# Retention followed by an RWKV channel mix: block 5 in 64-token chunks, keys turned and state summed in one pass, and a new order of all pieces

## The chip, the cores and the metric

The kernel runs on one core of a Trainium2 chip. The metric is the device time of one execution in microseconds (us). The five engines of the core run side by side, each through its own list of instructions in order, and wait for each other through semaphores: TensorE (PE, matrix products into the eight PSUM banks), VectorE (DVE), ScalarE (ACT), GpSimd (POOL) and SyncE (SP). POOL and SP issue most of the transfers here.

## What is computed

Cut to what matters, with B = 4 batches, H = 8 heads, S = 768 tokens, D = 64:

```python
gamma = 1.0 - 2.0 ** (-5.0 - np.arange(H))
for t in range(S):                                   # a recurrence for each head
    state = gamma * state + einsum('bhd,bhe->bhde', k[:, :, t], v[:, :, t])
    y[:, :, t] = einsum('bhd,bhde->bhe', q[:, :, t], state) / np.sqrt(D)
x = y.transpose(0, 2, 1, 3).reshape(B, S, H * D)     # 512 features a token
xk = mu_k * x + (1 - mu_k) * x_prev                  # x_prev: the token before
xr = mu_r * x + (1 - mu_r) * x_prev
k = np.maximum(xk @ w_k, 0)                          # 512 -> 1024
out = sigmoid(xr @ w_r) * ((k * k) @ w_v)            # 1024 -> 512
```

## The kernel before

The 3072 tokens are cut into twelve blocks of 256, three to a batch: blocks 0 to 2 are batch 0, 3 to 5 batch 1, and so on. The recurrence is done by chunks: inside a chunk as a masked score matrix times the values, from chunk to chunk through a 64x64 state for each head. Blocks of the table HALF (6 to 11) use 64-token chunks; blocks of WIDE (2 to 5) have 128 consecutive tokens as one tile, blocks 0 and 1 have tokens that alternate.

Nothing is scheduled by rule. The string ORDER (line 25) lists every piece of work as `code.block.part`, with `~v`, `~a`, `~p`, `~s` for DVE, ACT, POOL and SP, and `@` for the PSUM banks. The loop at the end of the kernel emits the pieces in that order, and each engine runs its own in that order. The codes that the text below uses:

- `lq`, `lk`, `lv`: load q, k, v of a block; `wk`, `wr`, `wv`: load the weights; `st`: store an output tile. Tiles of q, k and v lie in rings of four buffers, `vs` in a ring of three.
- `Tq`, `Tk` (PE) turn q and k; `Eq`, `Ek` (ACT) bring them out of PSUM. `turned_k` and `trans` have two forms: by 128-row tiles (blocks of WHOLE) or by 64x64 quarters.
- `vs` scales v by the decay (line 253). `S` (PE) makes the scores, `M` masks them on DVE (line 354, for half blocks line 347). `C` (PE) makes a chunk's state, `U` adds the carried state on DVE (line 419), `G` decays it for the next block (ACT).
- `I` and `J` (PE, line 441) multiply the carried states by q, `Y` (PE) the masked scores by v, all into the same two banks. For blocks that aren't wide, `Y` contains what `J` does. `D` on DVE (line 514, for half blocks line 507) brings the result to the buffer xT.
- `dx` (line 529) and `X` (lines 552, 558) make xk and xr: four `X.n.0.j` and four `X.n.1.j` for a block or a pair of blocks. Pairs (3, 4), (6, 7) and (9, 10) share their pieces.
- `K` (PE): xk times w_k, in pieces of 0.87 us; `Qa`, `Qb` (ACT): relu and square. `R` (PE): xr times w_r; `s` (ACT): sigmoid. `V` (PE): times w_v; `O` on DVE (line 630): product with the gate.
- `z` (PE): products of zeros into an unused bank, in the first 19 us only. `gy`: a table of decays that `D` multiplies by.

So `I.4` is the piece in which PE multiplies block 4's carried states by its q. It reads the result of `U.4.0`, the first DVE sum of block 4's state. `K.0.0` is the first piece of the channel mix.

The four lists that the change touches stand at the top of the kernel:

```python
HALF = (6, 7, 8, 9, 10, 11)
WHOLE = (0, 1, 2, 3)
WIDE = (2, 3, 4, 5)
```

Of the kernel before, what the change touches and what calls it, by code (L numbers as in the profile page):

```python
# [9 lines left out]
F16 = mybir.dt.float16  # L10
# [6 lines left out]
HALF = (6, 7, 8, 9, 10, 11)  # L17
# [15 lines left out]
K.0.2@1 Qa.0.0~a Qb.0.0~a Qa.0.2~a lq.3~p X.1.0.1~v X.1.0.3~v X.1.1.0~v Qa.0.1~a K.0.3@0 Qa.0.3~a
lk.3~p vs.2~v Tq.2@1 X.1.1.2~v K.1.3@6 K.1.0@0 C.2@7 U.2.0~v lv.3~p Eq.2~a S.2.1@23 M.2.1~v S.2.0@45
M.2.0~v Qb.0.3~a lv.4~p K.1.1@1 X.1.1.1~v Qa.1.0~a t.0.1.0~a K.1.2@7 I.2@23 Qb.0.1~a Qa.1.1~a wv.0~p
Qb.0.2~a Tq.4@01 Eq.4~a Y.2 Qa.1.3~a Qb.1.1~a X.0.1.3~v X.1.1.3~v R.1.1@4 Tk.4@01 Ek.4~a J.2 R.1.0@6
Qa.1.2~a s.1.0~a X.0.1.2~v X.0.1.1~v X.0.1.0~v R.0.1@5 s.0.1~a s.1.1~a R.0.0@7 s.0.0~a S.4.1@01
Qb.1.0~a D.2~v dx.2~v X.2.0.2~v X.2.0.0~v S.4.0@23 Tq.3@4 Eq.3~a X.2.0.1~v wv.1~p X.2.0.3~v Tk.3@7
lq.5~p Ek.3~a K.2.2@5 Qa.2.2~a K.2.3@4 M.4.1~v M.4.0~v Qa.2.3~a Qb.2.3~a lk.6~p S.3.1@67 M.3.1~v
S.3.0@01 vs.3~p C.3@23 U.3.0~a Qb.2.2~a K.2.1@4 Qa.2.1~a K.2.0@2 Qa.2.0~a I.3@45 lq.6~p vs.4~v  # L40
C.4@67 U.3.1~v X.2.1.1~v V.0.1.0@3 M.3.0~v V.1.0.0@2 G.3~a U.4.0~v I.4@01 X.2.1.3~v U.4.1~v J.3
Qb.1.3~a Y.4 Qb.2.0~a lk.5~p X.2.1.2~v X.2.1.0~v Y.3 D.3~v dx.3~v V.0.0.0@7 V.0.1.1 O.0.1~v Tq.5@45
J.4 D.4~v dx.4~v R.2.0@6 Qb.2.1~a V.0.0.1 O.0.0~v X.3.0.1~v Eq.5~a Qb.1.2~a V.1.0.1 X.3.0.2~v
O.1.0~v Tq.6@01 Eq.6~a Tk.6@45 Ek.6~a st.0.0~s lk.7~p st.1.0~s V.1.1.0@3 V.1.1.1 O.1.1~v s.2.0~a
# [36 lines left out]
"""
# [3 lines left out]
def kernel(  # L85
# [12 lines left out]
    nc = tc.nc  # L98
# [113 lines left out]
    def first(n):  # L212
        return n % NB == 0
# [586 lines left out]
```

## Time and profile before

| | |
|---|---|
| median of 3 runs | 153.35 us (153.19 to 153.39) |
| span of the profiled execution, first to last instruction | 151.4 us |
| PE busy | 143.4 us, 95% of the span |
| DVE busy | 127.8 us, 84% |
| ACT busy | 103.6 us, 68% |
| POOL busy | 55.3 us, 37% |
| granted PE clock | 1.000 |

The profile is of one execution, and the time of a run lies some 1.9 us above its span. A row of the timeline has the start, the length, the engine, the line, the tiles written and read, the shapes and the count of instructions; in brackets stands how long the engine was idle before it and what ended that. An instruction's own length is longer than its step: the next one starts before it ends, so steps are read from the starts of neighbouring rows.

### The profile page before, as it was taken

To read this page: it belongs to the slowest core of one execution; us is meant where nothing else is said; L and a number is where in the kernel's file an instruction comes from. 1 tells how busy PE (TensorE), PEld (TensorE's weight loads), DVE (VectorE), ACT (ScalarE), POOL (GpSimd) and SP (SyncE) were. 2 spreads that over 40 slices of the span, in tenths; PEclk is the share of its full clock that TensorE was granted. 3 is DMA by queue.
4 is the path that set the end of the run, shared out by engine and by line. 5 is a ranking of instruction groups with operands and counts; after the bars stand their busy time and mean duration, and the time that the engine had idled before them with its cause. 6 is when DMAs were issued, how large, how long until landed. Compare 5 with 4: busy or idle time off the path is not lost.

```text
span 151.4 us, 5541 instructions
## 1 busy us (share of the span) xinstructions
PE 143.4 (95%) x2426; PEld 82.8 (55%) x2426; DVE 127.8 (84%) x212; ACT 103.6 (68%) x195; POOL 55.3 (37%) x65
## 2 busy tenths in 40 slices
PE   7878799999999999999999999999999999999991
PEld 3345487757754554547465564548456444655450
DVE  7886999999989999999999999999799999400432
ACT  3565979899844795779567786999604756839420
POOL 7953998577957309996710000000000000000000
PEclk9999999999999999999999999999999999999999
DMA  5999999999999999999999019301000005500433
GB/s 140 219 229 197 207 231 192 168 251 212 196 167 202 233 262 107 256 300 198 231 173 126 7 38 283 105 35 45 0 4 0 4 0 211 205 0 0 148 133 139
DMA packets 45624, 22.16 MB, mean 146 GB/s; under 512 B 37400, under 2 KB 41248, under 8 KB 45600
## 3 DMA queue, kind: packets, MB, share of 16 engines
q0 software_dynamic: 38704, 14.42, 74.5%
q1 hardware_dynamic: 6592, 7.21, 14.3%
q8 instruction: 19, 0.31, 0.8%
q10 hardware_dynamic: 304, 0.18, 0.4%
q14 instruction: 5, 0.04, 0.1%
HBM read 24.16 MB, written 6.29 MB: 201 GB/s over the span
## 4 chain that ended last, share of the span: by engine, by line
PE 73%; DMA 12%; POOL 11%; issue 1%; DVE 0%; POOLq 0%
PE ps L624 27%; PE ps L572 14%; DMA v<-in_v_dram 12%; PE ps L612 12%; PE ps L582 8%; PE ps L278 3%; POOL q L235 3%; POOL k L230 2%; PE ps L441 2%; POOL vs L253 2%; POOL v L230 2%; PE ps L366 1%; PE ps L462 1%; PE ps L642 1%; PE ps L318 1%
## 5 line engine op out<-in xcount | busy, mean ns | idle before, releaser
L624 PE MATMUL ps<-wv,k2s 128*128 128x512 f16 x184 | 44.1, 380 | 0.0
L591 ACT ACTIVATE kr<-ps 128x512 f32<-128x512 f32 x48 | 27.9, 594 | 12.5 <-PE ps L582 6.5
L624 PEld LDWEIGHTS <-k2s 128*128 128x128 f16 x184 | 17.1, 98 | 18.9 <-ACT k2s L603 0.4
L630 DVE SCALAR_TENSOR_TENSOR os<-ps,rs 128x512 f32<-128x512 f32 x23 | 15.6, 684 | 11.9 <-ACT rs L618 9.4
L612 PE MATMUL ps<-wr,xr 128*128 128x512 f16 x96 | 23.5, 379 | 0.0
L582 PE MATMUL ps<-xk,wk 128*128 128x256 f16 x192 | 23.2, 273 | 0.0
L572 PE MATMUL ps<-xk,wk 128*128 128x512 f16 x96 | 23.0, 379 | 0.0
L618 ACT ACTIVATE rs<-ps 128x512 f32<-128x512 f32 x24 | 13.6, 597 | 12.9 <-PE ps L612 12.1
L230 POOL DMA_DIRECT2D k<-in_k_dram x20 | 17.8, 903 | 10.3 <-PE ps L384 6.7
L582 PEld LDWEIGHTS <-wk 128*128 128x128 f16 x192 | 18.1, 98 | 3.7
L241 ACT COPY qT<-ps 128x1024 f16<-128x1024 f16 (+1 forms) x13 | 12.3, 946 | 9.5 <-PE ps L278 7.8
L558 DVE SCALAR_TENSOR_TENSOR xr<-dx,mu,xT 128x256 f16<-128x256 f32 (+1 forms) x32 | 17.9, 577 | 0.1
L230 POOL DMA_DIRECT2D v<-in_v_dram x18 | 16.0, 911 | 3.6 <-DMA wr<-in_moe_w_r_dram 1.9
L558 DVE SCALAR_TENSOR_TENSOR xk<-dx,mu,xT 128x256 f16<-128x256 f32 (+1 forms) x32 | 17.0, 579 | 0.2
L354 DVE TENSOR_TENSOR a<-ps,c_sb 128x1024 f16<-128x1024 f32 (+1 forms) x14 | 14.6, 1066 | 0.9 <-PE ps L339 0.6
L603 ACT ACTIVATE k2s<-kr 128x512 f16<-128x512 f32 x24 | 14.8, 631 | 0.3
L612 PEld LDWEIGHTS <-xr 128*128 128x128 f16 x96 | 9.0, 97 | 10.7 <-issue 0.5
L572 PEld LDWEIGHTS <-wk 128*128 128x128 f16 x96 | 9.1, 98 | 10.5
L599 ACT ACTIVATE k2s<-kr 128x512 f16<-128x512 f32 x24 | 14.5, 627 | 0.3
L241 ACT COPY kT<-ps 128x1024 f16<-128x1024 f16 (+1 forms) x13 | 12.2, 945 | 2.2 <-PE ps L272 1.7
L529 DVE TENSOR_TENSOR dx<-xT 128x1024 f32<-128x1024 f32 x11 | 13.4, 1221 | 0.2
L253 DVE TENSOR_TENSOR vs<-v,csm_sb 128x1024 f16<-128x1024 f32 x10 | 12.2, 1217 | 0.2 <-DMA v<-in_v_dram 0.2
(73 smaller groups left out, 165.6 us busy)
## 6 DMA issues: line engine op xcount, KB each, us to landing
out_dram<-os SPq DMA_DIRECT2D x23, 256.0 KB, 2.4
v<-in_v_dram POOLq DMA_DIRECT2D x18, 256.0 KB, 7.7
q<-in_q_dram POOLq DMA_DIRECT2D x11, 256.0 KB, 8.4
k<-in_k_dram POOLq DMA_DIRECT2D x21, 128.0 KB, 8.8
v<-in_v_dram POOLq DMA_DIRECT2D x2, 512.0 KB, 7.2
wk<-in_moe_w_k_dram POOLq DMA_DIRECT2D x2, 512.0 KB, 10.4
wv<-in_moe_w_v_dram POOLq DMA_DIRECT2D x2, 512.0 KB, 10.4
wr<-in_moe_w_r_dram POOLq DMA_DIRECT2D x1, 512.0 KB, 8.7
```

The costliest lines, as they stand in the source:

```text
L230: e.dma_start(out=dst[:, :, i * D : i * D + D], in_=src[:, i * P : i * P + P].rearrange("h p d -> p h d"),)
L241: e.copy(out=out, in_=in_)
L253: e.tensor_tensor(out=VS(n), in0=V32(n).rearrange("p h (i d) -> p i h d", i=2), in1=gks[:, int(half(n) or wide(n)), :, :, None].to_broadca ...
L354: nc.vector.tensor_tensor(out=a_full(n)[:, i, :, j0:j1], in0=pairs(banks("S", n, i, j0))[:, :, j0:j1], in1=(below if wide(n) else causal[: ...
L558: nc.vector.scalar_tensor_tensor(out=XM[w](k)[:, j, t0:t1], in0=DX(k)[:, j, t0:t1], scalar=mu[:, w * NCO + j : w * NCO + j + 1], in1=x[:, ...
L572: nc.tensor.matmul(banks("K", n, g), lhsT=wk16[:, co, g * P : g * P + P], rhs=XM[0](k)[:, co, :], start=(co == 0), stop=(co == NCO - 1),)
L582: nc.tensor.matmul(pz[:, i, :], lhsT=wk16[:, co, fo * P : fo * P + P], rhs=XM[0](k)[:, co, m * TM + t0 : m * TM + t1], start=(i == 0 and c ...
L591: nc.scalar.activation(out=kr, in_=banks("K", n, g, *u), func=AF.Relu)
L603: nc.scalar.activation(out=K2(n)[:, w * g : w * g + w, t0:t1], in_=kr.rearrange("p a t -> p (a t)").rearrange("p (i t) -> p i t", i=w), fu ...
L612: nc.tensor.matmul(banks("R", n, tb), lhsT=XM[1](k)[:, co, t : t + P], rhs=wr16[:, co, :], start=(co == 0), stop=(co == NCO - 1),)
L624: nc.tensor.matmul(banks("V", n, tb), lhsT=K2(n)[:, fo, tb * P : tb * P + P], rhs=wv16[:, fo, :], start=(fo == 0), stop=(fo == NFO - 1),)
L630: nc.vector.scalar_tensor_tensor(out=OS(2 * n + tb), in0=banks("V", n, tb), scalar=1.0 / (KSC * KSC), in1=RS(2 * n + tb), op0=ALU.mult, op ...
```

## The change

Block 5 moves from WIDE to HALF, so it has four 64-token chunks. Block 4 is added to WHOLE, so its q and k are turned by 128-row tiles. For blocks 5 to 11 (MERGED) the pieces `Tk` and `C` are replaced by `TC.n.0` and `TC.n.1`: each k quarter is loaded once as the stationary operand, and an identity and the scaled v stream past it side by side (128 columns), so one product leaves the turned k and the state next to each other in fp32. `Ec` (two a block, ACT) takes the turned k out, `U` reads the state beside it. An identity stands ahead of each scaled v for that, which is three more small DVE instructions at the start.

A piece `w.n` (ACT) copies 16 elements of a row out of the banks of `I.n`, after `I.n` and ahead of `Y.n`, so that `Y.n` waits for the copy. The ring of gates has six buffers in place of four, that of outputs eight in place of four, xT two in place of three. ORDER is new from start to end; w_k comes in three parts (`wk.2.4`, `wk.1.2`, `wk.0.1`) in place of two.

```diff
-HALF = (6, 7, 8, 9, 10, 11)
+HALF = (5, 6, 7, 8, 9, 10, 11)
-WHOLE = (0, 1, 2, 3)
-WIDE = (2, 3, 4, 5)
+WHOLE = (0, 1, 2, 3, 4)
+WIDE = (2, 3, 4)
+MERGED = (5, 6, 7, 8, 9, 10, 11)
...
+    def VS(n):
+        return VI(n)[:, 1:].rearrange("p (i h) d -> p i h d", i=2)
...
-    VS = ring("vs_", 3, [2, H, D], F16)
+    VI = ring("vs_", 3, [2 * H + 1, D], F16)
...
-    RS = ring("rs_", 4, [dm], F32)
-    OS = ring("os_", 4, [dm], F32)
+    RS = ring("rs_", 6, [dm], F32)
+    OS = ring("os_", 8, [dm], F32)
...
+    def both(n, i):
+        return banks("TC", n, i).rearrange("p u (j x t) -> p u j x t", j=NJ, x=2)
+
+    def turned_state(e, n, i):
+        ps = both(n, i)
+        for j in range(NJ):
+            for u in range(2):
+                for a, h, jo, hp in heads(j):
+                    k = 1 + i * H + h
+                    x = slice(0, 2) if more(n) or not (u and i) else slice(0, 1)
+                    nc.tensor.matmul(
+                        ps[low(a), u, j, x], lhsT=K16(n)[low(u), h, i * D : i * D + D],
+                        rhs=VI(n)[low(u), 0 : k + 1 : k][:, x],
+                        start=(j == 0), stop=(j == NJ - 1), skip_group_check=True,
+                    )
+
+    def turned_k_part(e, n, i):
+        copy(
+            e, KT(n)[:, :, i].rearrange("c j (u p) -> c u j p", u=2), both(n, i)[:, :, :, 0],
+        )
...
+        if merged(n):
+            src = both(n, c // 2)[:, c % 2, :, 1]
...
+    def fence(e, n):
+        us = slice(0 if half(n) or not first(n) else 1, 2)
+        e.copy(out=fenced[:, us], in_=pairs(banks("I", n))[:, us, :, 0:C:W])
...
-    def load_wk(e, h):
-        f = slice(h * dff // 2, (h + 1) * dff // 2)
+    def load_wk(e, a, b):
+        f = slice(a * dff // 4, b * dff // 4)
```

The new order shows best on the instruction lists. First POOL, from the load of block 1's v on: `vs_1` is the scaling of block 1's v, which waits for that load, and everything below it is issued after it. Before:

```order
L235 DMA v32_1_71<-in_v_dram 128x8x128
L230 DMA k16_2_68<-in_k_dram 128x8x64 x2
L735 DMA wk16_127<-in_moe_w_k_dram 128x4x512 x2
L253 ISA
L253 TENSOR_TENSOR vs_1_75<-v32_1_71,csm_sb_121 128x1024
L235 DMA q16_2_64<-in_q_dram 128x8x128
L230 DMA v32_2_72<-in_v_dram 128x8x64 x2
L235 DMA q16_0_62<-in_q_dram 128x8x128
L738 DMA wr16_129<-in_moe_w_r_dram 128x4x512
L230 DMA k16_0_66<-in_k_dram 128x8x64 x2
```

And now:

```order
L244 DMA v32_1_71<-in_v_dram 128x8x128
L239 DMA v32_2_72<-in_v_dram 128x8x64 x2
L772 DMA wk16_133<-in_moe_w_k_dram 128x4x512
L262 ISA
L262 TENSOR_TENSOR vs_1_75<-v32_1_71,csm_sb_127 128x1024
L239 DMA k16_2_68<-in_k_dram 128x8x64 x2
L244 DMA q16_2_64<-in_q_dram 128x8x128
L772 DMA wk16_133<-in_moe_w_k_dram 128x4x256
L244 DMA q16_0_62<-in_q_dram 128x8x128
L772 DMA wk16_133<-in_moe_w_k_dram 128x4x256
L239 DMA k16_0_66<-in_k_dram 128x8x64 x2
L775 DMA wr16_135<-in_moe_w_r_dram 128x4x512
```

Block 2's k and half of w_k moved from ahead of the scaling to behind it; the load of block 3's v (`v32_3`) follows these rows directly. Further down POOL's list before there is a second scaling, that of block 3's v; now there is none.

Second DVE, from the last `dx` of batch 0 to `U.4.0`, which is the row that writes `tg2_1`. Before, from behind the four `X.2.0.j`:

```order
L354 TENSOR_TENSOR a2_1_84<-ps_61,c16_sb_120 128x1024 x2
L354 TENSOR_TENSOR a2_0_83<-ps_61,c16_sb_120 128x1024
L253 TENSOR_TENSOR vs_1_75<-v32_0_70,csm_sb_121 128x1024
L419 TENSOR_TENSOR t32_0_86<-ps_61,tg2_0_93 128x256
L558 SCALAR_TENSOR_TENSOR xr_2_106<-dx_0_99,mu_125,xT0_130 128x256
L354 TENSOR_TENSOR a2_0_83<-ps_61,c16_sb_120 128x1024
L419 TENSOR_TENSOR tg2_1_94<-ps_61,tg0_1_88 128x256
```

Now, from behind the first `X.2.0.j`:

```order
L262 TENSOR_TENSOR vs_0_74<-v32_3_73,csm_sb_127 128x1024
L363 TENSOR_TENSOR a2_1_84<-ps_61,c16_sb_126 128x1024
L594 SCALAR_TENSOR_TENSOR xk_2_103<-dx_0_99,mu_131,xT0_136 128x256 x3
L594 SCALAR_TENSOR_TENSOR xr_2_106<-dx_0_99,mu_131,xT0_136 128x256
L363 TENSOR_TENSOR a2_1_84<-ps_61,c16_sb_126 128x1024
L594 SCALAR_TENSOR_TENSOR xr_2_106<-dx_0_99,mu_131,xT0_136 128x256
L451 TENSOR_TENSOR t32_0_86<-ps_61,tg2_0_93 128x256
L262 TENSOR_TENSOR vs_1_75<-v32_0_70,csm_sb_127 128x1024
L363 TENSOR_TENSOR a2_0_83<-ps_61,c16_sb_126 128x1024
L594 SCALAR_TENSOR_TENSOR xr_2_106<-dx_0_99,mu_131,xT0_136 128x256 x2
L363 TENSOR_TENSOR a2_0_83<-ps_61,c16_sb_126 128x1024
L451 TENSOR_TENSOR tg2_1_94<-ps_61,tg0_1_88 128x256
```

The scaling of block 3's v (`vs_0<-v32_3`) has come over from POOL, and all four `xr_2` rows (the `X.2.1.j`) now stand ahead of `U.4.0`, where there was one.

On PE, the pieces that stand ahead of `I.4` are the same in both lists, with these exceptions: two `V` pieces (V.0.1.0 and V.1.0.0) were ahead of it and now follow it, `R.2.0` followed it and is now ahead, and the `z` pieces at the start are others. Ahead of `Y.0`, PE turns block 1's q and k in both lists; before, a `z` piece stood between the last score of block 0 and those turns, now none does. `Y.1` now follows directly on `I.1`, where the other half of block 1's scores, a turn and a `z` piece stood between them. `K.0.2` in place of `K.0.0` is the first piece of the channel mix.

More of the change, by code (lines that the diff above doesn't have):

```diff
@@ L164 @@
     wr16 = const.tile([P, NCO, dm], F16, name="wr16")
-    xT = [const.tile([P, NJ, COLS], F32, name=f"xT{b}") for b in range(B - 1)]
+    xT = [const.tile([P, NJ, COLS], F32, name=f"xT{b}") for b in range(2)]
     ident = c16[:, 0:P]
@@ L213, in first, with merged @@
         return n % NB == 0
+    def merged(n):
+        return n in MERGED
     def more(n):
@@ L406, in summed @@
     def summed(e, n, c):
[L407 to L410 removed]
+        last = c == (3 if half(n) else 1)
+        if merged(n):
+            src = both(n, c // 2)[:, c % 2, :, 1]
+        elif half(n):
+            src = banks("C", n)[:, c % 2, c // 2 * NJ * D : (c // 2 + 1) * NJ * D]
         else:
+            src = banks("C", n)
             src = (src[:, c] if more(n) else src)[:, 0 : NJ * D]
[L413 to L414 removed]
+        if not merged(n):
+            src = src.rearrange("p (j d) -> p j d", j=NJ)
         to = T32(n) if last else carried(n, c + 1)
@@ L677, in masks @@
             ((causal[:, 0], 1, ALU.is_ge), (causal[:, 1], 1, ALU.is_gt)),
-            ((step, 2, ALU.is_ge), (below, 0, ALU.is_ge)),
+            ((step, 2, ALU.is_ge), (below, 0, ALU.is_ge))
+            + tuple((VI(i)[:, 0], 2, ALU.is_equal) for i in range(3) if MERGED),
         )[part]:
```

128 lines of the change are left out of this document (62 added, 66 removed).

## Prediction

> **What bounds the kernel now.** I read the 40 slices of the page first, then the busy time by stretches, then the timelines of PE, DVE and POOL up to 43 us.
>
> ```profile
> PE   7878799999999999999999999999999999999991
> DVE  7886999999989999999999999999799999400432
> PEclk9999999999999999999999999999999999999999
> DMA  5999999999999999999999019301000005500433
> 13.95:42.59 28.64, 26.93 (x490) 18.86 (x489) 28.10 (x42) 25.66 (x50) 23.43 (x25) 1.00 1.50 206
> 42.59:148.24 105.65, 105.65 (x1757) 57.81 (x1756) 88.81 (x136) 70.72 (x131) 22.94 (x26) 1.00 0.71 123
> ```
>
> PE is full from about 19 us to the end, and at full clock. But DVE is full too, from slice 5 to slice 33, and the DMA engines are full up to 83 us. The last two rows are stretches (length, then the busy time of PE, PEld, DVE, ACT and POOL, the clock, DMA). From 13.95 to 42.59 us DVE is busy 28.10 of 28.64 us; from 42.59 on PE is busy all of 105.65 us and DVE has room. So a shorter PE list helps only behind the first stretch, and in the first stretch any added DVE work or DVE wait counts in full. The two limits are my stages, and the place where they hand over is `I.4`, which starts at 42.59 us:
>
> ```profile
> 41.90 0.42 DVE L419 TENSOR_TENSOR tg<-ps,tg 128x256 f16<-128x256 f32 x1 [0.20 <-ACT tg L424]
> 40.76 1.90 PE L624 MATMUL ps<-wv,k2s 128*128 128x512 f16 x8
> 42.59 0.42 PE L441 MATMUL ps<-qT,tg 64*64 64x128 f16 x12
> ```
>
> The first row is `U.4.0`; it ends at 42.32. PE has two V pieces until 42.59, then `I.4` and `J.3`. So the DVE chain and PE reach this point within 0.3 us of each other. The span ends 3.2 us after PE's last product at 148.24; the order of the last pieces (two V, a half-width V piece, its product with the gate, its store) is the same in kind, so I leave that, and the 1.9 us from span to median, as they are.
>
> **The start: D.0 comes about 0.55 us earlier.** These rows carry it (DVE, then PE, then POOL):
>
> ```profile
> 13.95 1.23 DVE L514 TENSOR_TENSOR xT<-ps,gy_sb 128x1024 f32<-128x1024 f32 x1 [1.19 <-PE ps L441]
> 10.87 1.89 DVE L354 TENSOR_TENSOR a<-ps,c_sb 128x512 f16<-128x512 f32 x3 [0.60 <-PE ps L339]
> 11.61 0.59 PE L710 MATMUL ps<-zero 128*128 128x512 f16 x2 [0.80 <-DVE a L354]
> 8.34 0.41 PE L272 MATMUL ps<-c_sb,k 128*64 128x128 f16 x8 [0.20 <-DMA k<-in_k_dram]
> 12.13 0.64 PE L272 MATMUL ps<-c_sb,q 128*64 128x128 f16 x16
> 12.60 0.61 PE L272 MATMUL ps<-c_sb,k 128*64 128x128 f16 x16
> 13.14 0.64 PE L489 MATMUL ps<-a,vs 64*64 64x128 f16 x32
> 4.65 0.90 POOL L235 DMA_DIRECT2D k<-in_k_dram  x1
> 5.52 0.92 POOL L235 DMA_DIRECT2D v<-in_v_dram  x1
> 13.66 1.90 POOL L253 TENSOR_TENSOR vs<-v,csm_sb 128x1024 f16<-128x1024 f32 x1 [3.98 <-DMA v<-in_v_dram]
> ```
>
> D.0 waits for `Y.0` (13.14 to 13.9), which stands behind `Tk.1` (12.60). In the new order the zeros ahead of `Tq.1` are gone, so `Tq.1` can run at about 11. `Tk.1` then waits for block 1's k. That load is issued just ahead of block 1's v, whose landing released POOL at 13.66; the second half of block 0's k landed at 8.3 (row at 8.34), and between then and 13.6 four loads (0.25, 0.5, 0.5 and 0.5 MB in HBM), so block 1's k lands one half-megabyte ahead, at about 12.1. Then `Tk.1` 0.54 us (12.60 to 13.14), `Y.0` and the way to DVE 0.81 (13.14 to 13.95): D.0 at 13.4. The three added identities and the late `gy` table lie on DVE while it waits anyway (0.20 us for v, 0.60, 1.19 in the rows of DVE); uncovered they would cost some 0.6 us.
>
> **From D.0 to U.4.0: DVE gets longer by 2.3 us.** One stretch of DVE without a wait gives all the steps, from start to start:
>
> ```profile
> 31.07 1.22 DVE L514 TENSOR_TENSOR xT<-ps,gy_sb 128x1024 f32<-128x1024 f32 x1
> 32.32 1.22 DVE L529 TENSOR_TENSOR dx<-xT 128x1024 f32<-128x1024 f32 x1
> 33.58 1.67 DVE L558 SCALAR_TENSOR_TENSOR xk<-dx,mu,xT 128x256 f16<-128x256 f32 x4
> 35.17 3.54 DVE L354 TENSOR_TENSOR a<-ps,c_sb 128x1024 f16<-128x1024 f32 x3
> 38.63 1.22 DVE L253 TENSOR_TENSOR vs<-v,csm_sb 128x1024 f16<-128x1024 f32 x1
> 39.76 0.42 DVE L419 TENSOR_TENSOR t<-ps,tg 128x256 f32<-128x256 f32 x1
> 40.09 0.48 DVE L558 SCALAR_TENSOR_TENSOR xr<-dx,mu,xT 128x256 f16<-128x256 f32 x1
> ```
>
> D 1.25, dx 1.26, X 0.40, M 1.15, vs 1.13, U 0.33. Before, from D.0 up to `U.4.0`: 3 D, 2 dx, 8 M, 2 vs, 4 U, 21 X = 3.75 + 2.52 + 9.20 + 2.26 + 1.32 + 8.40 = 27.45 us. The trace has 41.90 - 13.95 = 27.95, so waits made 0.5 of it. Now: the same, plus block 3's `vs` (1.13, which POOL did before, beside the rest) and three more `X.2.1.j` (1.20): 29.8 us. With the same half microsecond of waits, `U.4.0` starts at 13.4 + 29.8 + 0.5 = 43.7 and ends at 44.1, and `I.4` starts there. Without any wait it is 43.6.
>
> Does PE get there sooner by itself? Before, from `K.0.0` at 19.47 to `I.4` are 23.1 us. `K.0.2` should start near 19.05: D.0 at 13.4, two M, four X and one U are 4.25 us, so the last `X.0.0.j` ends near 18.9, and `Y.1` stands behind `I.1`, behind `w.1` and so behind `U.1.0`, which costs PE about half a microsecond there. From `K.0.2` to `I.4` the V pieces are missing (-1.83, 40.76 to 42.59), `Tk.2` is added (0.57, as 12.60 to 13.14), so is `R.2.0` (0.96), and block 4's two turns by 128-row tiles cost 0.5 each where quarters took 0.27 (+0.45): 23.25, so PE could be there at 42.3. That is 1.8 us before DVE, and PE must wait it out. This is also where PE's waits for late loads vanish: up to 1.8 us of them is covered.
>
> `I.4` thus moves from 42.6 to 44.1: +1.5 us.
>
> **From I.4 to the end: PE's list, about +0.4 us.** Ahead of `I.4` PE has lost two V pieces that now come behind it: +1.83. `R.2.0` is off this side, and block 5 is cheaper:
>
> ```profile
> 46.28 1.04 PE L612 MATMUL ps<-wr,xr 128*128 128x512 f16 x4
> 47.15 1.89 PE L624 MATMUL ps<-wv,k2s 128*128 128x512 f16 x8
> 55.94 0.62 PE L331 MATMUL ps<-qT,kT 64*128 64x128 f16 x16
> 56.49 0.32 PE L384 MATMUL ps<-vs,k 128*64 128x64 f16 x8
> 70.14 0.45 PE L318 MATMUL ps<-qT,kT 64*64 64x64 f16 x32
> 70.41 0.44 PE L462 MATMUL ps<-a,vs 64*64 64x64 f16 x32
> ```
>
> `R.2.0` is 0.87 (46.28 to 47.15). Block 5's scores go from 0.55 (55.94 to 56.49) to 0.27 (70.14 to 70.41); with its `Y`, `I` and `J` by the same pace I put the saving at 0.4 to 0.7. The merge: `Tk` and `C` of a half block are 32 products of 64 columns each, 0.27 each by the pace of these rows; `TC` is 32 products of 128 columns. The nearest row with 64x64 quarters and 128 columns is `Y.0`, 32 in 0.48 us (13.14 to 13.62). So 0.54 becomes 0.48 a block, six blocks (beside block 5): -0.4 at most, 0 if the two-piece moving operand costs anything. Sum: 1.83 - 0.87 - 0.55 - 0.2 = +0.2 by the middle values, between -0.15 and +0.6; each `TC` also stands alone among the large products more often than a `Tk` next to a `C` did, and each such switch of tile form costs PE about 0.1 us (four large products take 0.87 by the two rows at 46.28 and 47.15, so eight would take 1.74, while the eight ahead of `I.4` took 42.59 - 40.76 = 1.83). I take +0.4.
>
> The Trainium skill has another price for the merge: "TensorE: Matmul & The Clock Gate", under "Wait — 56ns, not 53.3ns?", says that starts of products never come closer than about 25 ns however few columns they have. By it 64 products would take 1.6 us and the merge would save 0.8 us a block. The trace disagrees: 32 products in 0.27 us are 8.4 ns each.
>
> The copies `w` cost PE nothing but at `Y.1`, since at least 0.5 us of other products stand between `I.n` and `Y.n`; on ACT they are twelve short copies, and `Ec` adds 14 copies of half size for 7 full ones, some 4 us in all on an engine that is busy 103.6 of 151 us. If they weren't covered, each would cost PE about 0.5 us, 5 in all at worst. The larger rings release DVE's products with the gate; DVE has room there, so nothing.
>
> **Sum.** 153.35 + 1.5 + 0.4 = **155.2 us**. Its own range is 154.2 (no waits on DVE, and the lower end behind `I.4`) to 156.2.
>
> **Rivals.** *DVE doesn't decide, PE does* (chance 0.17): `I.4` starts when PE is ready, at 42.3, by -0.3; behind it -0.15 to +0.6. That gives 152.9 to 153.7, and below 153.0 if `K.0.2` starts before 19. For it speaks that the two limits lie 0.3 us apart today; against it, the added 2.3 us are counted instructions with measured steps, and DVE had only 0.5 us of waits to lose. It decides if DVE covers D.0 to `U.4.0` in under 28 us. *Products paced by the instruction, not the column* (0.05): if a `TC` product keeps the 8.4 ns of a 64-column one, seven blocks save 0.27 each, 1.9 us: 153.3. Against it stands the row of `Y.0`, 15 ns each at 128 columns. *Late loads* (0.18, slower than my forecast): POOL's list behind block 1's scaling now holds block 2's k, the quarters of w_k, wr and then block 3's v.
>
> ```profile
> 15.51 0.95 POOL L235 DMA_DIRECT2D q<-in_q_dram  x1
> 16.45 1.79 POOL L230 DMA_DIRECT2D v<-in_v_dram  x2
> 19.07 0.82 POOL L738 DMA_DIRECT2D wr<-in_moe_w_r_dram  x1
> v<-in_v_dram POOLq DMA_DIRECT2D x18, 256.0 KB, 7.7
> ```
>
> The nine issues ahead of block 3's v take 0.75 to 0.95 each by these rows, so it is issued at 23.4 and 24.3 and lands 7.7 us later, near 32. DVE wants it after 3 D, 2 dx, 4 M, 1 vs, 3 U and 17 X, 19.8 us by the steps above, at 33.2. With the DMA engines full it may land 1 to 3 us later, and DVE then waits with everything behind it, for the whole 1 to 2 us: 156.2 to 157.5. It decides from a landing at 33.7 on. The rest (0.60) is the forecast.
>
> **Range and chances.** The likeliest is 155.2. The forecast's range with the late loads reaches 157.2 upward, and downward I take in most of the PE rival: 153.1 to 157.2. About 0.2 % (0.3 us) is what a measurement of this kernel can tell. Slower by more than that: all of the forecast, late loads, and a small part of the PE rival, 0.80. Within: 0.09, from the PE rival and the paced products. Faster: 0.11, from the same two.
>
> **What would show it.** In the changed kernel D.0 (the first DVE product with the `gy` table over 128x1024) near 13.4; from it to the DVE sum ahead of `I.4` 29.8 to 30.5 us with DVE nearly full; PE with 1.5 to 2.5 us of idle time between `K.0.2` (near 19) and `I.4` (near 44); PE full from there on, for about 106 us. A `TC` piece should take 0.23 to 0.25 us. I am wrong if `I.4` starts before 43, if PE idles more than 1 us behind it, or if D.0 is not near 13.4.

## The result, and the profile after

| | kernel before | changed kernel |
|---|---|---|
| median | 153.27 us of 4 runs (153.00 to 153.39) | 157.21 us of 4 runs (156.10 to 158.36) |
| ratio | 1 | 1.0249, 95% interval 1.0205 to 1.0293 |
| profiled execution | span 151.4 us | 157.17 us, span 155.4 us |
| PE busy | 143.4 us | 146.0 us |
| I.4 starts | 42.59 us | 46.12 us |
| from I.4 to PE's last product | 105.65 us | 105.96 us |

The changed kernel is 2.5% slower, by 3.9 us. Medians and ranges here and below are of all executions of a kernel, while a ratio leaves out those that lie over 1.5% above the fastest of their kernel (one of e2_vs3_on_pool, one of e9_first_of_before, two of e11_first_mended), so it need not be the ratio of two medians.

First the page of the changed kernel: busy time, then the slices (40 equal parts of the span) of PE, DVE, the granted clock and the transfers.

```profile
PE 146.0 (94%) x2260; PEld 82.6 (53%) x2260; DVE 128.7 (83%) x217; ACT 104.1 (67%) x214; POOL 55.9 (36%) x67
PE   7998765999999999999999999999999999999991
DVE  7897996989999999999999998999899995601242
PEclk9999999999999999999999999999999999999999
GB/s 142 214 224 231 129 134 174 206 211 252 206 197 228 165 203 60 295 193 223 158 218 172 126 292 6 6 104 35 4 4 0 0 79 128 0 202 0 202 101 169
```

The same row of transfer rates for the kernel before:

```profile
GB/s 140 219 229 197 207 231 192 168 251 212 196 167 202 233 262 107 256 300 198 231 173 126 7 38 283 105 35 45 0 4 0 4 0 211 205 0 0 148 133 139
```

Counted from 0, slices 4 and 5 (15.5 to 23.3 us) carry 129 and 134 GB/s where they carried 207 and 231. There the transfers have a hole, and PE has one right behind it, 6 and 5 tenths in slices 5 and 6. The busy times of the two stretches, from D.0 to I.4 and on to PE's last product (length, then PE, PEld, DVE, ACT, POOL, the clock, DMA share and rate), place the loss:

```profile
13.62:46.12 32.50, 28.34 (x457) 19.11 (x455) 30.12 (x46) 24.87 (x54) 25.12 (x28) 1.00 1.43 190
46.12:152.08 105.96, 105.96 (x1625) 57.47 (x1624) 87.49 (x135) 72.29 (x148) 22.90 (x26) 1.00 0.69 119
```

The first stretch took 28.64 us before and takes 32.50 now, and PE idles 4.2 us of it. Behind I.4 PE is full, for 0.3 us more. PE's timeline of the changed kernel says what it waited for:

```profile
19.55 1.92 PE L618 MATMUL ps<-xk,wk 128*128 128x256 f16 x16
21.40 0.64 PE L281 MATMUL ps<-c_sb,k 128*64 128x128 f16 x16
24.40 0.64 PE L281 MATMUL ps<-c_sb,q 128*64 128x128 f16 x16 [2.37 <-DMA q<-in_q_dram]
25.80 1.05 PE L618 MATMUL ps<-xk,wk 128*128 128x256 f16 x8 [0.76 <-DMA wk<-in_moe_w_k_dram]
45.16 1.02 PE L648 MATMUL ps<-wr,xr 128*128 128x512 f16 x4
46.12 0.42 PE L473 MATMUL ps<-qT,tg 64*64 64x128 f16 x12
```

It waited 2.37 us for block 2's q (Tq.2), then 0.76 us for w_k (K.0.1). DVE, which is the engine that the prediction watched, waits as well, behind PE:

```profile
27.21 0.42 DVE L451 TENSOR_TENSOR tg<-ps,tg 128x256 f16<-128x256 f32 x1 [1.47 <-PE ps L393]
31.95 1.22 DVE L546 TENSOR_TENSOR xT<-ps,gy_sb 128x1024 f32<-128x1024 f32 x1 [0.72 <-ACT kr L627]
```

The first row is U.2.0, which needs block 2's state, and that stood on PE behind the late pieces. The second is D.2. The view puts its wait down to ACT, but D.2 also needs J.2, which PE ran from 31.54 to 31.85 us. Why the loads are late stands in POOL's timeline:

```profile
8.16 0.83 POOL L772 DMA_DIRECT2D wk<-in_moe_w_k_dram  x1
14.12 1.90 POOL L262 TENSOR_TENSOR vs<-v,csm_sb 128x1024 f16<-128x1024 f32 x1 [5.13 <-DMA v<-in_v_dram]
15.97 1.82 POOL L239 DMA_DIRECT2D k<-in_k_dram  x2
17.76 0.90 POOL L244 DMA_DIRECT2D q<-in_q_dram  x1
18.63 0.79 POOL L772 DMA_DIRECT2D wk<-in_moe_w_k_dram  x1
```

From 9.0 to 14.1 us POOL waits for block 1's v, in order to scale it, and scales until 16.0. Everything below it is issued only then. What had been issued ahead has landed by 18.6 us, and the rate of the transfers falls meanwhile:

```profile
17.00:18.00 1.00, 1.00 (x6) 0.35 (x3) 1.00 (x3) 0.38 (x1) 1.00 (x2) 1.00 0.58 72
```

The last figure is 72 GB/s. In the kernel before, the same microsecond has 207.

### The profile page after: what moved, and what is told of

The parts are those of the page before. It is cut to its first block, busy times and chain, and to the rows that moved or that the text cites. A ratio compares the mean times of both kernels' runs of the same rounds, so it can differ in the third digit from the quotient of the medians.

```text
span 155.4 us, 5244 instructions
## 1 busy us (share of the span) xinstructions
PE 146.0 (94%) x2260; PEld 82.6 (53%) x2260; DVE 128.7 (83%) x217; ACT 104.1 (67%) x214; POOL 55.9 (36%) x67
## 4 chain that ended last, share of the span: by engine, by line
PE 74%; DMA 10%; POOL 5%; DVE 5%; ACT 3%; issue 1%; POOLq 0%
PE ps L660 26%; PE ps L608 14%; PE ps L648 11%; PE ps L618 10%; DMA v<-in_v_dram 5%; DMA wk<-in_moe_w_k_dram 5%; PE ps L422 3%; PE ps L473 2%; POOL q L244 2%; PE ps L494 1%; PE ps L327 1%; ACT qT L250 1%; PE ps L287 1%; POOL k L239 1%; PE ps L678 1%
## 5 line engine op out<-in xcount | busy, mean ns | idle before, releaser
L618 PE MATMUL ps<-xk,wk 128*128 128x256 f16 x192 | 24.3, 273 | 0.9 <-DMA wk<-in_moe_w_k_dram 0.8
L648 PE MATMUL ps<-wr,xr 128*128 128x512 f16 x96 | 24.0, 379 | 0.0
L239 POOL DMA_DIRECT2D v<-in_v_dram x20 | 18.0, 918 | 9.8 <-DVE vs L262 7.1
L262 DVE TENSOR_TENSOR vs<-v,csm_sb 128x1024 f16<-128x1024 f32 x11 | 13.4, 1218 | 0.5 <-DMA v<-in_v_dram 0.5
L244 POOL DMA_DIRECT2D q<-in_q_dram x12 | 10.7, 894 | 5.8 <-PE ps L287 4.9
L363 DVE TENSOR_TENSOR a<-ps,c_sb 128x1024 f16<-128x1024 f32 (+1 forms) x12 | 12.2, 1040 | 0.2 <-PE ps L348 0.2
```

The costliest lines, as they stand in the source:

```text
L239: e.dma_start(out=dst[:, :, i * D : i * D + D], in_=src[:, i * P : i * P + P].rearrange("h p d -> p h d"),)
L618: nc.tensor.matmul(pz[:, i, :], lhsT=wk16[:, co, fo * P : fo * P + P], rhs=XM[0](k)[:, co, m * TM + t0 : m * TM + t1], start=(i == 0 and c ...
L648: nc.tensor.matmul(banks("R", n, tb), lhsT=XM[1](k)[:, co, t : t + P], rhs=wr16[:, co, :], start=(co == 0), stop=(co == NCO - 1),)
```

## Experiments

Each ran beside fresh runs of the kernel before, whose medians lay between 153.26 and 153.37 us.

| | median, us | range | ratio to before, 95% |
|---|---|---|---|
| e1_loads_ahead | 154.67 | 154.37 to 155.21 | 1.0085 (1.0067 to 1.0103) |
| e2_vs3_on_pool | 156.97 | 155.78 to 159.33 | 1.0218 (1.0176 to 1.0260) |
| e3_both | 154.48 | 154.36 to 154.77 | 1.0066 (1.0049 to 1.0082) |
| e4_k2_late_in_before | 159.40 | 159.05 to 160.97 | 1.0401 (1.0367 to 1.0434) |
| e5_prefix | 155.41 | 154.88 to 156.98 | 1.0157 (1.0117 to 1.0197) |
| e7_zeros | 159.67 | 159.48 to 160.51 | 1.0422 (1.0402 to 1.0442) |
| e10_zeros_sized | 158.16 | 157.92 to 158.22 | 1.0321 (1.0303 to 1.0338) |
| e8_zeros_in_after | 157.29 | 156.97 to 157.59 | 1.0257 (1.0240 to 1.0274) |
| e12_zeros_in_after_sized | 156.23 | 156.14 to 158.29 | 1.0213 (1.0167 to 1.0258) |
| e9_first_of_before | 159.02 | 157.94 to 161.84 | 1.0346 (1.0313 to 1.0380) |
| e11_first_mended | 156.44 | 155.62 to 159.07 | 1.0176 (1.0145 to 1.0207) |

### The three loads, and the scaling of block 3's v

```diff
-lv.2~p wk.2.4~p t.0.0.3~a z.2@0 S.1.1@45 vs.1~p M.1.1~v ... M.1.0~v lk.2~p
-z.5@1 C.1@01 ... w.1~a lq.2~p Y.1 ... X.0.0.0~v wk.1.2~p
+lv.2~p wk.2.4~p lk.2~p lq.2~p wk.1.2~p t.0.0.3~a z.2@0 S.1.1@45 vs.1~p M.1.1~v ... M.1.0~v
+z.5@1 C.1@01 ... w.1~a Y.1 ... X.0.0.0~v
```

> The changed kernel, with three loads (block 2's k, block 2's q, the second part of w_k) moved on POOL from behind the scaling of block 1's v to ahead of it; nothing else differs. Theory (late loads): the scaling waits for block 1's v until 14.0 us, so these loads are issued only from 16.0 on and land at 21.1, 24.4 and 25.8 us; PE waits 2.6 us for block 2's q and 1.0 us for w_k. Issued some 6 us earlier they land before PE asks for them, PE reaches I.4 as early as DVE's list lets it, near 44.2 us in place of 46.1, and the time falls from 157.2 to about 155.3. Rival (DVE's longer list alone makes the loss, and PE's waits are covered): I.4 stays within 0.5 us of 46.1 and the time within 0.5 us of 157.2. Second rival (the transfers only change places: what is pulled ahead pushes block 1's v back): the scaling ends later than 17 us, block 1's state is late, and the time gains less than 0.8 us.

154.67 us: three moved loads give 2.5 of the 3.9 us back. POOL and PE of this kernel:

```profile
8.91 1.85 POOL L239 DMA_DIRECT2D k<-in_k_dram  x2
10.65 0.98 POOL L244 DMA_DIRECT2D q<-in_q_dram  x1
11.84 0.76 POOL L772 DMA_DIRECT2D wk<-in_moe_w_k_dram  x1 [0.21 <-issue]
13.46 1.90 POOL L262 TENSOR_TENSOR vs<-v,csm_sb 128x1024 f16<-128x1024 f32 x1 [0.85 <-DMA v<-in_v_dram]
...
18.76 1.92 PE L618 MATMUL ps<-xk,wk 128*128 128x256 f16 x16
21.90 0.64 PE L281 MATMUL ps<-c_sb,q 128*64 128x128 f16 x16 [0.65 <-DMA q<-in_q_dram]
23.26 1.05 PE L618 MATMUL ps<-xk,wk 128*128 128x256 f16 x8 [0.72 <-DMA wk<-in_moe_w_k_dram]
43.28 0.42 PE L473 MATMUL ps<-qT,tg 64*64 64x128 f16 x12
```

The scaling starts no later than it did (13.46, where it was 14.12), so the second rival falls; I.4 is at 43.28, 0.9 us earlier than I had expected, so the first falls too. Some waiting is left: q and w_k still come 0.65 and 0.72 us late, probably because the transfers ahead of them fill the time, which no run shows by itself. Block 2's v, 0.5 MB, is loaded ahead of both and lies ready before DVE asks for it.

```diff
-Qb.1.2~a lv.4~p lv.5~p vs.3~v Qa.1.1~a
+Qb.1.2~a lv.4~p lv.5~p vs.3~p Qa.1.1~a
```

> The changed kernel, with block 3's scaling given back to POOL (it was moved to DVE); nothing else differs. It takes 1.1 us from DVE's list ahead of U.4.0. Theory (late loads decide, through PE): I.4 stays near 46 us and the time near 157, a gain under 0.4 us. Rival (the sum of DVE's list decides, as the prediction had it): I.4 comes 1.1 us earlier, near 45.0, and the time is near 156.1.

> Both edits: the three loads ahead of the scaling of block 1's v, and block 3's scaling on POOL. Theory (late loads first, DVE's list 1.5 us behind it): the loads alone bring I.4 to 44.2 us, and with DVE's list 1.1 us shorter it comes to about 43.1, the time to about 154.2: the second edit, worth nothing alone, is worth 1.1 us here. Rival (DVE's list never decided): no gain over the loads alone, about 155.3.

In the changed kernel alone the edit gives nothing that can be told (156.97, with a range of 155.78 to 159.33), which fits the theory. It is no clean proof, though. DVE and POOL of e2_vs3_on_pool show that the edit did not take 1.1 us from DVE:

```profile
34.70 2.66 DVE L594 SCALAR_TENSOR_TENSOR xr<-dx,mu,xT 128x256 f16<-128x256 f32 x1
...
35.15 1.92 POOL L262 TENSOR_TENSOR vs<-v,csm_sb 128x1024 f16<-128x1024 f32 x1
```

An X piece, 0.48 us everywhere else, took 2.66 us beside POOL's scaling. So DVE lost 2.2 us there and saved 1.1. In e3_both the scaling fell beside an M piece (33.58 us, 1.23 us long, as always), so there the test is cleaner: DVE has 1.13 us less to do, and the time falls by 0.19 us, not by the 1.1 that I had expected. The sum of DVE's list does not set the time by itself even with the loads moved. The stretch from the first K piece to I.4 in the two kernels, e1_loads_ahead first:

```profile
18.76:43.28 24.52, 23.05 (x340) 16.51 (x336) 24.20 (x37) 20.10 (x41) 17.18 (x20) 1.00 1.53 208
...
19.69:43.67 23.98, 23.05 (x343) 16.55 (x337) 22.90 (x36) 20.11 (x41) 18.94 (x21) 1.00 1.51 208
```

With the scaling on DVE, DVE idles 0.3 us and PE 1.5 us. Without it the stretch is 0.54 us shorter, DVE idles 1.1 us and PE still 0.9. Counted from D.0, I.4 comes only 0.16 us earlier in these two executions: from D.0 to the first K piece e3_both took 0.38 us longer (13.58 to 19.69, where it was 13.03 to 18.76), with a longer wait of PE at C.1 (0.58 us where it was 0.16) that the edit does not explain. Even 0.54 us is half of what DVE was spared. DVE, PE and the transfers bound this stretch within 1 us of each other; taking from one of them alone gives little.

### A load put late in the kernel before

```diff
-lq.1~p lk.1~p z.2@3 S.0.1.2.4@23 U.0.1~v lv.1~p lk.2~p I.0@01 ...
-wk.1~p G.0~a z.2@6 Tq.1@6 Eq.1~a vs.1~p lq.2~p Tk.1@7 ...
+lq.1~p lk.1~p z.2@3 S.0.1.2.4@23 U.0.1~v lv.1~p I.0@01 ...
+wk.1~p G.0~a z.2@6 Tq.1@6 Eq.1~a vs.1~p lk.2~p lq.2~p Tk.1@7 ...
```

> The kernel before, with one load moved: block 2's k from ahead of w_k (issued at 6.4 us, landed at 15.6) to behind the scaling of block 1's v on POOL, where the changed kernel has it. Theory (a load behind that scaling is late): it is issued near 15.6 and lands near 20, PE waits for it at Tk.2 ahead of the first K piece, and since PE and DVE reach I.4 within 0.3 us of each other there, the wait is not covered: I.4 1.0 to 3.0 us later and a time of 154.3 to 156.3. Rival (PE has enough other work or DVE hides it): within 0.4 us of 153.3.

159.40 us, 6.0 us slower and twice my upper end. The mechanism is there: PE waits for k, and with it Y.1, which stands behind Tk.2 on PE, and D.1 on DVE. But something else is there. PE, then the stretches with the clock (the figure ahead of the DMA share), then D.1:

```profile
16.75 0.39 PE L339 MATMUL ps<-qT,kT 64*64 64x128 f16 x16
19.95 0.32 PE L272 MATMUL ps<-c_sb,k 128*64 128x128 f16 x2 [2.80 <-DMA k<-in_k_dram]
20.79 0.96 PE L272 MATMUL ps<-c_sb,k 128*64 128x128 f16 x14 [0.52 <-DMA k<-in_k_dram]
...
18.00:18.50 0.50, 0.00 (x0) 0.00 (x0) 0.50 (x2) 0.00 (x0) 0.50 (x1) 0.68 2.20 139
20.00:22.00 2.00, 1.48 (x17) 0.93 (x18) 0.00 (x0) 0.21 (x1) 2.00 (x3) 0.50 1.60 238
22.00:24.00 2.00, 2.00 (x43) 1.17 (x42) 0.00 (x0) 1.76 (x5) 2.00 (x4) 0.50 1.24 201
24.00:26.00 2.00, 2.00 (x15) 1.60 (x14) 1.93 (x2) 0.52 (x1) 2.00 (x3) 0.75 1.41 178
...
24.04 1.22 DVE L514 TENSOR_TENSOR xT<-ps,gy_sb 128x1024 f32<-128x1024 f32 x1 [4.43 <-PE ps L441]
```

The granted clock falls to half about 1.0 us into the wait and stays there until 25 us. All six executions have a mean clock of 0.978 or 0.979. That raised a question for the changed kernel too: its four runs had clocks of 1.000, 0.986, 0.987 and 1.000.

### Is it the clock?

```diff
-X.0.0.1~v t.0.1.2~a X.0.0.2~v Tk.2@0 t.0.1.3~a
+X.0.0.1~v t.0.1.2~a X.0.0.2~v z.24@4 Tk.2@0 t.0.1.3~a
```

> The kernel of e4_k2_late_in_before with six 512-column fp32 products of zeros into an unused bank put ahead of Tk.2, where PE waited 2.8 us for block 2's k; they take about 2.6 us and nothing new is computed. Theory (the wait itself made the half clock, 0.50 to 0.54 from 18 to 24 us there): the granted clock stays 1.00, PE's pieces between 20 and 25 us take half as long, D.1 comes 0.7 to 1.5 us earlier, and the time falls from 159.4 to 158.0 to 158.7. Rival (the half clock has another cause, or the later landing of block 2's q decides anyway): the time within 0.4 us of 159.4.

The clock was 1.00 in all, and the time 159.67 us, no better; but the zeros ran until 22.6 us, past the landing of the load, so the filler itself now held PE. With a shorter one (`z.13@4`):

> As e7_zeros, with zeros of the right length: one 512-column fp32 product took 0.89 us there, not the 0.43 that I had counted (each shows as two rows), so the six ran to 22.6 us, 1.8 us past the landing of block 2's k. Now three of them and an fp16 one, about 2.9 us, to 20.2. Theory (half clock after the wait costs time): the clock stays 1.00, D.1 starts near 22.9 us where it was 24.0 without zeros, and the time is 158.0 to 158.7 against 159.4. Rival (the half clock costs nothing, since loads decide anyway): within 0.3 us of 159.4.

158.16 us, 1.24 us less than without the zeros. D.1 of this kernel, and the stretch that had half a clock:

```profile
20.00:22.00 2.00, 1.35 (x20) 0.65 (x18) 0.00 (x0) 0.21 (x1) 2.00 (x3) 1.00 1.60 217
...
23.08 1.22 DVE L514 TENSOR_TENSOR xT<-ps,gy_sb 128x1024 f32<-128x1024 f32 x1 [3.27 <-PE ps L441]
```

PE does products of no use, nothing else is changed, and the kernel is faster by 1.2 us: the idle wait itself halved the clock, and the half clock cost time.

The other 4.9 us aren't all the late load. DVE, POOL and PE of e10_zeros_sized further on:

```profile
36.95 3.66 DVE L558 SCALAR_TENSOR_TENSOR xk<-dx,mu,xT 128x256 f16<-128x256 f32 x4
...
37.21 1.91 POOL L253 TENSOR_TENSOR vs<-v,csm_sb 128x1024 f16<-128x1024 f32 x1
...
47.58 0.42 PE L441 MATMUL ps<-qT,tg 64*64 64x128 f16 x12
```

The load makes D.1 3.3 us late (23.08, where it was 19.78). The four X pieces then take 3.66 us where they took 1.67, since POOL's scaling of block 3's v, beside M pieces in the kernel before, now falls beside them: 2.0 us more. Together that is the 5.0 us by which I.4 is late (47.58, where it was 42.59). In e4_k2_late_in_before the scaling falls beside `dx`, which takes 2.63 us in place of 1.22. So this kernel tests the late load together with a shifted scaling, and no run takes the two apart.

Now the same in the changed kernel, in both lengths:

```diff
-Tq.2@2 Eq.2~a
+z.16@5 Tq.2@2 Eq.2~a
```

> The changed kernel with four fp32 products of zeros ahead of Tq.2, inside the 2.4 us in which PE waits for block 2's q; nothing else differs. Theory (part of the loss is a clock that falls after that wait in some executions: 0.986 in two of four): every execution at a clock of 0.996 or more, all of them between 155.8 and 157.3 us, median 156.5. Rival (the clock is no matter here): the same spread as the changed kernel, clocks of 0.986 among them, a median of 157.2.

> The changed kernel with 2.0 us of zeros ahead of Tq.2 (two fp32 products and an fp16 one), where PE waits 2.4 us for block 2's q; in e8_zeros_in_after they ran 1.0 us past its landing. Theory (in some executions of the changed kernel the clock halves after that wait, which makes part of its spread from 156.1 to 158.4): every clock 0.996 or more, none above 157.5, median 156.2 to 156.8. Rival (the clock makes no difference to the end, since loads decide): median within 0.3 us of 157.2.

With the long filler (`z.16`) all clocks were 0.997 or more and the spread shrank to 156.97 to 157.59, but Tq.2 came at 25.44 us, 1.0 us later than in the changed kernel. With the short one (`z.9`) five of six executions lie between 156.14 and 156.62 us, the sixth at 158.29, all at 0.996 or more; the median is 156.23.

That is 1.0 us below the changed kernel, but it doesn't show that 1.0 us of the loss is clock. The intervals of the two ratios overlap. The changed kernel's two executions at full clock took 157.17 and 156.10 us, those at 0.986 and 0.987 took 158.36 and 157.25. And in the profile of e12_zeros_in_after_sized w_k is there 11.6 us behind D.0, so that PE doesn't wait for it, where it landed 12.2 us behind D.0 in the changed kernel's: landings differ between executions too. The clock's share of the median loss stays open. That the clock does fall in this order, a trace shows: e2_vs3_on_pool, the same up to there, was profiled in an execution with a mean clock of 0.986:

```profile
24.00:26.00 2.00, 1.24 (x18) 0.90 (x16) 1.38 (x4) 1.01 (x1) 1.79 (x3) 0.92 1.65 189
26.00:28.00 2.00, 2.00 (x29) 1.49 (x26) 1.19 (x2) 0.00 (x0) 1.11 (x2) 0.50 2.15 172
28.00:30.00 2.00, 2.00 (x18) 1.42 (x19) 2.00 (x4) 0.95 (x2) 0.65 (x1) 0.72 1.39 206
```

It was at half from about 25.7 to 29.1 us, right behind PE's waits of 1.82 us at Tq.2 and 0.76 us at K.0.1. The profile of the changed kernel has a clock of 1.00 and took 157.17 us, so its loss of 3.9 us is all waits.

### Parts of the list moved further

```diff
-... vs.1~p M.1.1~v ...
-D.1~v vs.2~v dx.1~v Tq.2@2 Eq.2~a X.0.1.0~v X.1.0.0~v K.0.1@0 C.2@1 wk.0.1~p S.2.1@67 X.1.0.3~v
-S.2.0@45 X.1.0.1~v X.1.0.2~v K.1.3@2 K.1.0@3 X.1.1.1~v Qa.1.3~a lk.4~p U.2.0~v
+... vs.1~p vs.2~p M.1.1~v ...
+D.1~v dx.1~v Tq.2@2 Eq.2~a X.0.1.0~v X.1.0.0~v C.2@1 S.2.1@67 X.1.0.3~v
+S.2.0@45 X.1.0.1~v X.1.0.2~v K.1.3@2 K.0.1@0 K.1.2@3 X.1.1.1~v Qa.1.3~a lk.4~p wk.0.1~p U.2.0~v
```

> The kernel of e3_both with block 2's scaling on POOL too (behind that of block 1), the K piece that waits for w_k moved behind K.1.3, K.1.0 and K.1.2 exchanged so that the last part of w_k is needed later, and block 4's k loaded ahead of that part. Theory (what decides is DVE's list up to the last X piece ahead of K.1.3, then PE's list of 18.2 us from K.1.3 to I.4; DVE's sum up to U.4.0 decides nothing any more): taking block 2's scaling out of that first part brings K.1.3 from about D.0 + 12.0 us to about D.0 + 10.6, and the time from 154.5 to about 153.6. Rival (the end of DVE's list or the transfers still decide): I.4 stays at about D.0 + 30.1 us and the time at 154.5.

155.41 us, slower than e3_both by 0.9. K.1.3 came at D.0 + 11.7, not + 10.6: what was taken from DVE came back as the X pieces that ran beside POOL's scalings. Three of them took 2.25 us in place of 1.26 beside the first, and beside the other, DVE and POOL of this kernel:

```profile
32.88 2.30 DVE L594 SCALAR_TENSOR_TENSOR xk<-dx,mu,xT 128x256 f16<-128x256 f32 x1
...
32.98 1.92 POOL L262 TENSOR_TENSOR vs<-v,csm_sb 128x1024 f16<-128x1024 f32 x1
```

So my account of the stretch (DVE's list up to K.1.3, then PE's) was not tested by this and stays an argument.

```diff
-WHOLE = (0, 1, 2, 3, 4)
+WHOLE = (0, 1, 2, 3)
...
-Tq.4@1 Qb.0.2~a Qb.0.3~a w.2~a Tk.4@2 M.2.1~v
+Tq.4@12 Qb.0.2~a Qb.0.3~a w.2~a Tk.4@67 M.2.1~v
```

> The kernel of e5_prefix with block 4's q and k turned by quarters again, as before the change. Theory (PE's list decides here): 2 x 0.22 us less on PE ahead of I.4, so 0.3 to 0.45 us less than e5_prefix, near 153.2. Rival (DVE or the loads decide): within 0.15 us of e5_prefix.

In this kernel block 4's turned k is written over block 2's scores before they are masked, so it computes something else; its 159.41 us say nothing of the quarters.

The next kernel has the order of the kernel before up to I.4, and of the changed kernel's order what is left. Its own pieces, the kernel before being the minus side:

```diff
-I.4@01 X.2.1.3~v U.4.1~v J.3 Qb.1.3~a Y.4 ... Y.3 D.3~v dx.3~v V.0.0.0@7 V.0.1.1 O.0.1~v Tq.5@45 J.4 D.4~v
+I.4@01 w.4~a X.2.1.3~v U.4.1~v J.3 Qb.1.3~a Y.3 ... D.3~v Y.4 J.4 ... D.4~v V.0.0.0@7 V.0.1.1 dx.3~v
...
+R.2.1@0 s.2.1~a TC.5.1@45 Ec.5.1~a X.3.0.3~v TC.5.0@06 Ec.5.0~a G.4~a U.5.0~v U.5.1~v O.1.0~v K.3.0@7
```

> The order of the kernel before up to I.4 (block 4 turned by quarters, w_k in two parts, block 5's v and k loaded where block 6's k and q were), then the changed kernel's pieces, merged and with block 5 in 64-token chunks; between I.4 and K.3.0 an order of its own. Theory (the change loses only ahead of I.4, and behind it is cheaper by what was moved there): I.4 at 42.6 us as before, then 106.0 us of the changed kernel's PE list less the two V pieces that are done ahead (1.83) and with R.2.0 (0.87) behind: 105.0 us where the kernel before has 105.65, so about 152.7 us. Rival (DVE, which then has three X pieces and block 5's scaling to do between I.4 and K.3.0, makes PE wait there): 0.5 to 2 us of PE's idle time ahead of K.3.0 and 153.3 to 154.7 us. Second rival (merging and 64-token chunks gain nothing on PE): 153.4 us with PE full.

I.4 came at 42.75 us and K.3.0 at 52.95, as wanted, and then PE waited 2.29 us at K.3.7 for a product with the gate that I had put behind a late sum on DVE; the clock halved after it, 159.02 us in the median. Mended (`O.0.1` also moves behind K.3.7):

```diff
-V.1.0.1 vs.5~v Qb.2.1~a R.2.0@6 s.2.0~a Tq.5@45 ... R.2.1@0 s.2.1~a TC.5.1@45
-... Ec.5.0~a G.4~a U.5.0~v U.5.1~v O.1.0~v K.3.0@7
+V.1.0.1 vs.5~v Qb.2.1~a G.4~a R.2.0@6 s.2.0~a R.2.1@0 s.2.1~a Tq.5@45 ... TC.5.1@45
+... Ec.5.0~a O.1.0~v K.3.0@7 U.5.0~v U.5.1~v
```

> As e9_first_of_before, with its own fault taken out: there PE waited 2.3 us at K.3.7 for O.1.0, which stood on DVE behind the sums of block 5's state, which waited for the decay of block 4's (G.4) on ACT; and its clock halved after that wait. Now G.4 stands 5 us earlier, O.1.0 ahead of those sums, R.2.1 next to R.2.0. Theory (behind I.4 the changed kernel is cheaper by what was moved there, and no more): PE reaches K.3.7 at 53.5 to 54.1 us, 95.7 us less R.2.1 (0.9) to its end, a clock of 1.00, and 153.1 to 154.0 us: no measurable gain over the kernel before. Rival (the merge and the 64-token chunks are worth 0.6 us more): under 152.8. Second rival (the order behind K.3.7 doesn't bear DVE's being later): over 154.5.

156.44 us: the second rival. PE of this kernel:

```profile
42.98 0.42 PE L482 MATMUL ps<-qT,tg 64*64 64x128 f16 x12
54.39 1.02 PE L617 MATMUL ps<-xk,wk 128*128 128x512 f16 x4 [0.46 <-DVE os L675]
64.03 1.02 PE L617 MATMUL ps<-xk,wk 128*128 128x512 f16 x4 [0.17 <-ACT kr L636]
106.38 0.72 PE L627 MATMUL ps<-xk,wk 128*128 128x256 f16 x5 [0.66 <-issue]
```

With the start of the kernel before, I.4 is back at 43.0 us, but from K.3.7 on PE needs 96.8 us where the changed kernel needed 95.7 and, without R.2.1, about 94.7 were left to do. PE waits for 1.2 of these 96.8 us and is busy for 0.8 more than the 94.7, which nothing here explains. Whether the merge and the 64-token chunks are worth something in an order made for them stays open. No kernel here beats the one before.

## Why the prediction was right, and where not

The forecast was 155.2 us in a range of 153.1 to 157.2; 157.21 came out. The direction is right, and so is the place: nearly all of it is lost ahead of I.4, 3.5 us there and 0.3 us from there to PE's last product. The forecast was a loss of 1.9 us, and 3.9 came: the size is off by a step that failed. The result lies at the very top of the range, and that top came from the rival of late loads with the wrong load, so that it reached so far is in part luck.

- **Start.** D.0 at 13.4 was predicted; 13.62 in the profiled run, 13.03 and 13.58 in e1_loads_ahead and e3_both. The first K piece near 19.05: 19.55, 18.76 and 19.69. Right to 0.4 and 0.6 us; the executions differ by 0.6 and 0.9. PE waits for block 1's k ahead of Tk.1, as predicted (to 12.20 us, where 12.1 was said).
- **DVE's list, 29.8 us and half a microsecond of waits.** In e1_loads_ahead, where DVE hardly waits, U.4.0 starts at 42.51, 29.5 us behind D.0, and DVE is busy for 29.2 of them. The sum with its waits was 0.8 us too long, and it was not what decided: 1.13 us less of it gave 0.19 us (e3_both). In the changed kernel it is 31.7 us from D.0 to U.4.0, with DVE idle for 2.4 of them: the waits that the sum put at 0.5.
- **PE's list, 23.25 us from the first K piece to I.4.** In e1_loads_ahead 24.52 less waits of 0.65 and 0.72: 23.15. Right.
- **"Up to 1.8 us of PE's waits for late loads is covered."** This step failed, twice. The waits for loads were 3.1 us at Tq.2 and K.0.1, above the 1.8, and PE idled 3.4 us between the first K piece and I.4 where 1.5 to 2.5 were expected. And what is covered must not feed the cover: U.2.0 on DVE needs block 2's state from PE, so PE's wait made DVE wait 1.47 us at 27.21, and the two lists were late together. Moving three loads took 2.84 us from I.4 (46.12 to 43.28; 2.25 of them counted from D.0) and 2.5 us from the time.
- **The rival of late loads** had 156.2 to 157.5 us and the right line of POOL, the scaling of block 1's v, but the wrong load: block 3's v, at the end of the list behind that scaling, for which DVE did not wait. PE waited for the second and third entries of that list, block 2's q and the second part of w_k; the first, block 2's k, stood ahead of both. I had their issue order before me and followed only the last.
- **The clock** was taken as 1.00 throughout. Two of the changed kernel's four executions were at 0.986 and 0.987; what that costs the median stays open (between nothing and about 1 us by the runs with filler products).
- **Behind I.4: +0.4 us.** 105.96 against 105.65: +0.3, and 105.97 and 105.96 in e1_loads_ahead and e3_both. Right as a sum; none of its terms was tested alone.
- **TC and w.** Two TC pieces side by side took 0.57 us with the switch of tile form behind them:

```profile
52.39 0.63 PE L422 MATMUL ps<-vs,k 64*64 64x128 f16 x32
52.96 2.76 PE L660 MATMUL ps<-wv,k2s 128*128 128x512 f16 x12
18.86 0.64 PE L521 MATMUL ps<-a,vs 64*64 64x128 f16 x32 [0.33 <-ACT fenced L554]
```

  so 0.24 each and 0.1 for the switch, as predicted. The last row is Y.1: 0.33 us for the copy where I had said about 0.5, and in the whole trace it is the only wait of PE for one of the twelve copies.

That the products aren't paced by the instruction (the rival at 0.05) these rows show too: 32 products of 128 columns in about 0.5 us.

## What to carry to other kernels

When an order is rewritten, take each queue that both computes and issues transfers, and ask for every load below a computing instruction when that instruction can start; the first loads below it are the ones at risk. A wait on one engine is covered by another only if the other needs nothing that comes after the wait. And a late load can cost more than its wait: PE's clock may halve in it, which filler products of the right length took back in one kernel here (1.2 us), and what POOL computes later may fall beside another DVE piece that it stops.

## What the runs showed of the hardware

**The clock falls within a short wait.** In e4_k2_late_in_before PE's last product ended near 17.1 us and the clock was at half from about 18.2 to 25.0 us, though PE worked again from 19.95 on. In e2_vs3_on_pool it was at half from about 25.7 to 29.1 us, behind waits of 1.82 and 0.76 us. The Trainium skill ("TensorE: Matmul & The Clock Gate", "What's actually happening") says that the clock is halved after at least one idle window of about 3.4 us, a window that runs freely. The halving fits that, and so do the two lengths, some 6.8 and 3.4 us; an idle window does not: of the 3.4 us up to the fall PE was busy for 1.70 us in the one case and for 1.52 us in the other, so a window need not be wholly idle. Such a wait doesn't always do it either: the profiled execution of the changed kernel kept its clock with PE busy for 0.67 of 3.4 us (22.0 to 25.4 us). Where the window falls would explain that; no run here shows it.

**POOL's scaling stops DVE pieces that read two tensors from SBUF.** An X piece of 0.48 us took 2.66 and 2.30 us beside a POOL instruction of 1.9, four of them 3.66 in place of 1.67, and a `dx` 2.63 in place of 1.22; M pieces beside it kept their 1.2 us (in the kernel before all three that ran beside block 3's scaling). X and `dx` read two tensors from SBUF, M one from SBUF and one from PSUM. The Trainium skill ("SBUF — State Buffer", "Who interferes with whom") has this rule: a DVE instruction with two SBUF inputs contends with a GpSimd instruction that reads SBUF, and the ports that the two share are locked for one of them at a time. The trace agrees: each of these DVE rows ends behind the end of POOL's, by 0.28 to 1.5 us. So the scaling that the change moved to DVE, +1.13 us in the prediction, was no pure loss: its cost on POOL depends on which DVE piece it meets.

**Products of zeros in fp32** of 512 columns took 0.89 us each (six in 5.35 us in e7_zeros) and show as two rows each.
